# Issuing the raw expert weight loads of an attention and mixture-of-experts kernel on POOL's DMA queue

## The chip, the cores and the metric

The kernel runs on one core of one Trainium2 chip. The core has a TensorE for matrix products (PE in the rows), a VectorE (DVE), a ScalarE (ACT), a GpSimd (POOL) and a SyncE (SP), each with an instruction stream of its own that runs in program order, and 16 DMA engines that move data between HBM and the on-chip memory. SP and POOL can both issue DMAs; the rows call SP's sequencer SPq. The metric is the device time of one execution in microseconds (us), as the median over several executions.

## What is computed

Three stages follow one another: sparse attention (a local window and a few global keys) over 4 batches, 8 heads, 768 positions and a head size of 64; a dense layer pair 512 to 2048 to 512 with an ELU between; and a mixture of 8 experts, of which each token uses at most one. The last is what the change touches:

```python
def _moe2_ref(x, w_skip, w_gate, w1, w2):
    do_compute = x @ w_skip > 0
    out = x.copy()
    xc = x[do_compute]
    logits = xc @ w_gate
    e_idx = np.argmax(logits, axis=1)
    ...
    for e in range(E):                       # 8 experts
        mask = e_idx == e
        h = np.maximum(xc[mask] @ w1[e], 0.0)            # w1[e]: 512 x 1024
        y[mask] = gate_w[mask, None] * (h @ w2[e])       # w2[e]: 1024 x 512
    out[do_compute] = xc + y
    return out
```

All inputs are float32. The kernel makes each matrix product out of three float16 products (high part by high part, high by low, low by high).

## The kernel before

The 3072 tokens pass through attention and the dense pair in 8 groups `m` of 384 tokens; a group takes 16 steps `f` (128 of the 2048 hidden columns each). In a step `moe_h` makes `h` (L441), ACT and DVE make the ELU, ACT its high half `gs[:, 0]` (L451), POOL its low half (L452), and two steps later `moe_y` multiplies it by the second weight (L462). Each group is then routed (`route`): its rows are written to a table `xg` in HBM, 256 rows for each expert, by an indirect DMA that POOL issues (L586).

Experts come last. Their raw weights arrive in 64 loads of 512 KB (`ex_load`): for expert `e`, loads `k` = 0 to 3 are `w1`, 4 to 7 are `w2`. Two consecutive loads share a tile `er` of the pool `stage`, which has two buffers, so a pair of loads waits until the pair before the last has been worked up. `ex_prep` works a load up in two halves: ACT writes the scaled high part (L627), DVE the low part (L628) of `ew`. When `prep()` takes the first half of a load `k` it first calls `ex_load` for `k + 2`. The first 32 halves (experts 0 and 1) are worked up during group 7 of the dense pair, the rest in `ex_tail`.

In `ex_tail` steps run over `(e, f, tiles)`: first experts 0 to 3 with their first 128 tokens (32 steps), then experts 0 to 3 with their second 128 (32 steps), then experts 4 to 6 with 256 tokens at once, then expert 7 in two halves. A step is `ex_first` (L665, result `eh`), ACT and DVE make `ehs` (L667, L669), and two steps later `ex_second` (L681, result `eo`). A step goes with one half of `prep`, from expert 4 on with two; steps 32 to 41 have none. Tokens are fetched from `xg` by SP (`ex_gather`, L640, tile `yg`), split by DVE into `eyh` (L649, L650; one buffer) and turned by a transposing DMA that SP issues (`ex_tokens`, L651, tile `eyT`). After an expert's last step DVE makes the rows `eres` (L689) and their row numbers `ix` (L691), and POOL scatters them to the output (L692).

The framework's scheduler decides the order in which each engine's instructions stand, except for those pinned to program order (`self.pin`); waits are on semaphores, and an engine or a queue that waits holds back all that stands behind it.

Of the kernel before, what the change touches and what calls it, by code (L numbers as in the profile page):

```python
# [64 lines left out]
class Fast:  # L65
# [538 lines left out]
    def ex_load(self, e, k):  # L604
        nc = self.nc
        w1 = self.a["moe2_w1"][e].rearrange("(c p) f -> p c f", p=P)
        w2 = self.a["moe2_w2"][e].rearrange("(g c p) d -> p g c d", p=P, c=2)
        if k % 2 == 0:
            self.es = self.stage(f"er_{e}_{k}")
        r = self.es[:, k % 2]  # L610
        if k < 4:
            nc.sync.dma_start(r, w1[:, k])
        else:
            nc.sync.dma_start(r.rearrange("p (c d) -> p c d", c=2), w2[:, k - 4])
        self.er[(e, k)] = r

    def ex_prep(self, e, k, j):
# [581 lines left out]
```

## Time and profile before

| | |
|---|---|
| three runs | 863.15 us median (861.58 to 864.68) |
| the profiled execution | 864.38 us, of which the span of its instructions is 862.6 us |
| PE busy | 819.2 us, 95% of the span |
| DVE, ACT, POOL busy | 571.3, 532.1 and 173.5 us |
| mean granted TensorE clock | 0.981 of full speed |
| SP's DMA queue (hardware_dynamic) | 141.59 MB, 60.7% of 16 DMA engines' span |
| POOL's DMA queue (software_dynamic) | 5.99 MB, 1.9% |

Times in the rows count from the span's start. A row of the timeline gives the start, the length, the engine, the line, the operation and how often it is repeated; in brackets stands how long the engine was idle before, and who ended that. POOL's 64 weight loads do not exist yet: what POOL issues before are 24 scatters to `xg` and 16 to the output.

### The profile page before, as it was taken

To read this page: it belongs to the slowest core of one execution; us is meant where nothing else is said; L and a number is where in the kernel's file an instruction comes from. 1 tells how busy PE (TensorE), PEld (TensorE's weight loads), DVE (VectorE), ACT (ScalarE), POOL (GpSimd) and SP (SyncE) were. 2 spreads that over 40 slices of the span, in tenths; PEclk is the share of its full clock that TensorE was granted. 3 is DMA by queue.
4 is the path that set the end of the run, shared out by engine and by line. 5 is a ranking of instruction groups with operands and counts; after the bars stand their busy time and mean duration, and the time that the engine had idled before them with its cause. 6 is when DMAs were issued, how large, how long until landed. Compare 5 with 4: busy or idle time off the path is not lost.

```text
span 862.6 us, 17864 instructions
## 1 busy us (share of the span) xinstructions
PE 819.2 (95%) x6329; PEld 479.1 (56%) x6329; DVE 571.3 (66%) x1967; ACT 532.1 (62%) x1318; POOL 173.5 (20%) x201
## 2 busy tenths in 40 slices
PE   6998989999999999999999999999999889989995
PEld 5774444555555555555555555555555666756663
DVE  7997996575566576656656756542677865867832
ACT  4775766777766677776767776644766443545421
POOL 1002112123123211321321232232241111100010
PEclk9998998999999999999999999999999899999998
DMA  8998983544686486578547755420656796578810
GB/s 299 268 276 259 245 218 90 118 111 105 184 230 172 127 195 146 154 195 217 160 133 179 166 137 153 93 64 13 174 182 178 209 308 175 186 219 249 244 44 25
DMA packets 185395, 148.80 MB, mean 173 GB/s; under 512 B 152209, under 2 KB 154257, under 8 KB 181201
## 3 DMA queue, kind: packets, MB, share of 16 engines
q1 hardware_dynamic: 182096, 141.59, 60.7%
q0 software_dynamic: 3200, 5.99, 1.9%
q8 instruction: 51, 0.84, 0.4%
q14 instruction: 48, 0.39, 0.2%
HBM read 94.82 MB, written 21.08 MB: 134 GB/s over the span
## 4 chain that ended last, share of the span: by engine, by line
PE 72%; DVE 11%; DMA 9%; issue 3%; ACT 1%; POOL 1%; SPq 1%; DVEq 0%; POOLq 0%; ACTq 0%
PE h L441 25%; PE y L462 23%; PE eh L665 6%; PE eo L681 6%; PE s L241 5%; PE pv L326 5%; DMA eyT<-eyh 4%; DVE wt L410 1%; PE warm L356 1%; DVE w L418 1%; DMA er<-in_moe_w 1%; DVE ew L628 1%; DVE wt L411 1%; DMA pT<-ph 1%; DVE p L250 1%
## 5 line engine op out<-in xcount | busy, mean ns | idle before, releaser
L441 PE MATMUL h<-xT,w 128*128 128x384 f16 x1536 | 276.1, 330 | 3.9 <-DMA xT<-xs 3.0
L462 PE MATMUL y<-w,gs 128*128 128x512 f16 x1152 | 271.9, 380 | 1.1 <-POOL gs L452 1.0
L452 POOL TENSOR_TENSOR gs<-e,gs 128x384 f16<-128x384 f32 x128 | 123.3, 966 | 431.7 <-ACT gs L451 361.3
L441 PEld LDWEIGHTS <-w 128*128 128x128 f16 x1536 | 147.3, 99 | 107.0 <-issue 11.2
L462 PEld LDWEIGHTS <-gs 128*128 128x128 f16 x1152 | 109.8, 98 | 121.5 <-POOL gs L452 4.2
L448 DVE SCALAR_TENSOR_TENSOR e<-e,h 128x384 f32<-128x384 f32 x128 | 70.3, 550 | 108.4 <-ACT e L446 104.5
L451 ACT ACTIVATE gs<-e 128x384 f16<-128x384 f32 x128 | 66.7, 522 | 78.6 <-DVE e L448 77.4
L255 ACT ACTIVATE p<-p,st 128x232 f32<-128x232 f32 (+1 forms) x192 | 89.3, 466 | 40.2 <-DVE st L250 39.9
L665 PE MATMUL eh<-eyT,ew 128*128 128x128 f16 (+1 forms) x1248 | 104.7, 235 | 8.8 <-DMA eyT<-eyh 5.3
L665 PEld LDWEIGHTS <-ew 128*128 128x128 f16 x1248 | 90.0, 99 | 36.0 <-DMA eyT<-eyh 6.7
L628 DVE SCALAR_TENSOR_TENSOR ew<-er,ew 128x512 f16<-128x512 f32 x128 | 91.6, 729 | 26.6 <-ACT ew L627 26.2
L681 PE MATMUL eo<-ew,ehs 128*128 128x512 f16 x384 | 101.9, 383 | 3.2 <-ACT ehs L667 1.5
L445 ACT ACTIVATE e<-h 128x384 f32<-128x384 f32 x128 | 61.8, 483 | 65.5 <-PE h L441 52.5
L667 ACT ACTIVATE ehs<-eh 128x128 f16<-128x128 f32 (+1 forms) x104 | 31.3, 301 | 91.5 <-PE eh L665 91.5
L627 ACT ACTIVATE ew<-er 128x512 f16<-128x512 f32 x128 | 75.9, 620 | 11.3 <-DMA er<-in_moe_w 11.3
L250 DVE CUSTOM_DVE_ANT_0 p<-s,tab 128x232 f32<-128x232 f32 (+1 forms) x192 | 67.0, 376 | 20.4 <-PE s L241 18.6
L285 DVE TENSOR_TENSOR ph<-p,ph 128x464 f16<-128x464 f32 x68 | 42.8, 644 | 41.0 <-ACT ph L284 41.0
L446 ACT ACTIVATE e<-e 128x384 f32<-128x384 f32 x128 | 66.7, 521 | 2.6
L669 DVE SCALAR_TENSOR_TENSOR ehs<-eh,ehs 128x128 f16<-128x128 f32 (+1 forms) x104 | 33.0, 318 | 36.9 <-ACT ehs L667 35.2
L692 POOL DMA_INDIRECT out<-eres,ix x16 | 18.0, 1124 | 167.8 <-DVE ix L691 78.6
L681 PEld LDWEIGHTS <-ehs 128*128 128x128 f16 x384 | 34.6, 99 | 28.6 <-DVE ehs L669 3.0
L241 PE MATMUL s<-qh 64*128 64x232 f16 (+1 forms) x432 | 40.2, 256 | 4.0 <-DVE st L250 3.0
(171 smaller groups left out, 849.1 us busy)
## 6 DMA issues: line engine op xcount, KB each, us to landing
er<-in_moe_w SPq DMA_DIRECT2D x64, 512.0 KB
wr<-in_wf SPq DMA_DIRECT2D x16, 1024.0 KB
wc<-in_wf SPq DMA_DIRECT2D x16, 1024.0 KB
qk<-in_qk SPq DMA_DIRECT2D x20, 720.0 KB
out<-yt SPq DMA_DIRECT2D x24, 256.0 KB
rawv<-in_vp SPq DMA_DIRECT2D x21, 256.0 KB
xg<-zrow SPq DMA_DIRECT2D x16, 257.0 KB
yg<-xg SPq DMA_DIRECT2D x16, 257.0 KB
```

Of the source, the lines that this page charges most:

```text
L241: nc.tensor.matmul(sp[j], q[r, hp, KW:], k[r, hp, KW - w:KW], start=(x == 0), stop=(x == len(mm) - 1))
L250: nc.vector.tensor_tensor_reduce(pw[:, j, :], sp[j], self.tab[:, h, :] if i else self.tab0[:, h, :], -0.125, 3e38, ALU.add, ALU.min, st[:, ...
L255: nc.scalar.activation(pw[:, j, :], pw[:, j, :], AF.Exp, bias=st[:, 0, h:h + 1], scale=-1.0, accum_out=st[:, 1, h:h + 1])
L441: nc.tensor.matmul(hps, wi[:, s_, c, :], xT[:, x * ND + c, :], start=(n == 0), stop=(n == 3 * ND - 1))
L446: nc.scalar.activation(e, e, AF.Relu, scale=-1.0, bias=1.0)
L448: nc.vector.scalar_tensor_tensor(g, e, -HS, hps, ALU.mult, ALU.max, accum_out=self.gsum[:, m * NF + f:m * NF + f + 1])
L452: nc.gpsimd.tensor_tensor(gs[:, 1], g, gs[:, 0], ALU.subtract)
L462: nc.tensor.matmul(self.ys[m][t], gs[:, s_, t * P:(t + 1) * P], wo[:, x, :], start=(f == 0 and n == 0), stop=(f == NF - 1 and n == 2))
L627: self.pin(nc.scalar.activation(w[:, 0], r, AF.Copy, scale=sc))
L628: nc.vector.scalar_tensor_tensor(w[:, 1], r, sc, w[:, 0], ALU.mult, ALU.subtract, accum_out=self.esums[:, c:c + 1])
L665: nc.tensor.matmul(hps, l, r, start=(i == 0), stop=(i == len(mm) - 1))
L681: nc.tensor.matmul(self.eo[(e, t)], hs[:, s_, j * P:(j + 1) * P], self.ew[(e, 4 + f // 2, f % 2)][:, x, :], start=(f == 0 and n == 0), sto ...
```

## The change

Both DMA calls in `ex_load` are issued by POOL instead of SP. The 64 loads, their sizes, their buffers and everything else stay.

```diff
@@ def ex_load(self, e, k): @@
         r = self.es[:, k % 2]
         if k < 4:
-            nc.sync.dma_start(r, w1[:, k])
+            nc.gpsimd.dma_start(r, w1[:, k])
         else:
-            nc.sync.dma_start(r.rearrange("p (c d) -> p c d", c=2), w2[:, k - 4])
+            nc.gpsimd.dma_start(r.rearrange("p (c d) -> p c d", c=2), w2[:, k - 4])
         self.er[(e, k)] = r
```

The scheduler places the loads anew. The first place is POOL's stream in steps 9 to 12 of the dense pair's group 7, where the loads of expert 1 (`er_4`, `er_6`) now stand between the low halves `gs` of four steps:

```order
 L452 TENSOR_TENSOR gs_9_8180<-e_9_8176,gs_9_8180 128x384
+L614 DMA er_4_8228<-in_moe_w 128x2x512 x2
 L452 TENSOR_TENSOR gs_10_8225<-e_10_8221,gs_10_8225 128x384
 L452 TENSOR_TENSOR gs_11_8270<-e_11_8266,gs_11_8270 128x384
+L614 DMA er_6_8280<-in_moe_w 128x2x512 x2
 L452 TENSOR_TENSOR gs_12_8313<-e_12_8309,gs_12_8313 128x384
```

A pair of loads, with its wait for a free buffer, stands ahead of every other `gs`.

The second place is around steps 10 to 17 of `ex_tail`. On POOL, the last loads of expert 2 (`er_6_8748`) and the first of expert 3 (`er_0_8880`, `er_2_8971`) now stand among the scatters:

```order
+L614 DMA er_6_8748<-in_moe_w 128x2x512 x2
 L692 DMA out<-eres_0_8799,ix_0_8801 3072x512
 L586 DMA xg<-yt_8547,pos_8459 2048x514
 L586 DMA xg<-yt_8550,pos_8459 2048x514
 L586 DMA xg<-yt_8553,pos_8459 2048x514
+L612 DMA er_0_8880<-in_moe_w 128x1024 x2
+L612 DMA er_2_8971<-in_moe_w 128x1024 x2
 L692 DMA out<-eres_0_9003,ix_0_9005 3072x512
```

All four loads of `w1` of expert 3 come behind the group's three scatters to `xg`. On SP the same loads are gone from among the output writes (L593) and the first gather of the second tokens (`yg_1_9080`), which waits for those scatters:

```order
-L612 DMA er_0_8880<-in_moe_w 128x1024
 L593 DMA out<-yt_8547 128x512
 L593 DMA out<-yt_8550 128x512
 L593 DMA out<-yt_8553 128x512
-L612 DMA er_0_8880<-in_moe_w 128x1024
 L640 DMA yg_1_9080<-xg 128x514
-L612 DMA er_2_8971<-in_moe_w 128x1024 x2
 L640 DMA yg_1_9082<-xg 128x514
```

Before, the third and fourth load of expert 3 stood behind that gather's wait.

The third place is DVE's stream just before expert 4's first step, where its second 128 tokens are split (`eyh_1_10056`):

```order
 L669 SCALAR_TENSOR_TENSOR ehs_5_1_10073,esums<-eh_5_1_10060,ehs_5_1_10073 128x128
 L628 SCALAR_TENSOR_TENSOR ew_1_1_10076,esums<-er_0_9895,ew_1_1_10076 128x512
+L649 TENSOR_SCALAR eyh_1_10056<-yg_1_9903 128x512
 L669 SCALAR_TENSOR_TENSOR ehs_6_1_10095,esums<-eh_6_1_10082,ehs_6_1_10095 128x128
-L649 TENSOR_SCALAR eyh_1_10056<-yg_1_9903 128x512
+L650 SCALAR_TENSOR_TENSOR eyh_1_10056<-yg_1_9903,eyh_1_10056 128x512
 L628 SCALAR_TENSOR_TENSOR ew_2_0_10100,esums<-er_2_9995,ew_2_0_10100 128x512
-L650 SCALAR_TENSOR_TENSOR eyh_1_10056<-yg_1_9903,eyh_1_10056 128x512
 L669 SCALAR_TENSOR_TENSOR ehs_7_1_10119,esums<-eh_7_1_10106,ehs_7_1_10119 128x128
```

The split stands one `ehs` and one `ew` earlier; for experts 5 and 6 it moves ahead of one `ew` in the same way.

## Rows read from the trace of the kernel before

**Rows 1.** The page: busy us, share of the span and instructions of PE.
```profile
PE 819.2 (95%) x6329; PEld 479.1 (56%) x6329; DVE 571.3 (66%) x1967; ACT 532.1 (62%) x1318; POOL 173.5 (20%) x201
```

**Rows 2.** Windows: stretch, PE, PEld, DVE, ACT, POOL busy, granted clock, DMA share, GB/s.
```profile
664.00:690.00 26.00, 22.66 (x236) 15.28 (x233) 22.13 (x112) 14.28 (x40) 4.29 (x4) 0.87 0.72 193
690.00:720.00 30.00, 26.90 (x294) 18.56 (x293) 21.04 (x91) 14.31 (x38) 3.36 (x4) 1.00 0.86 281
758.00:780.00 22.00, 18.07 (x123) 12.05 (x121) 12.84 (x46) 9.44 (x21) 0.97 (x1) 0.92 0.75 198
```

**Rows 3.** Timeline of PE after its three longest idle stretches of the expert stage.
```profile
673.59 1.44 PE L665 MATMUL eh<-eyT,ew 128*128 128x128 f16 x12 [2.99 <-DVE ehs L669]
...
764.74 5.77 PE L665 MATMUL eh<-eyT,ew 128*128 128x256 f16 x36 [3.49 <-DMA eyT<-eyh]
...
807.75 1.49 PE L665 MATMUL eh<-eyT,ew 128*128 128x256 f16 x12 [1.86 <-DMA eyT<-eyh]
```

**Rows 4.** PE's waits from 690 to 720 us: total us, times, longest.
```profile
PE eo L681 <- ACT ehs L667: 1.5, 1, 1.5
PE eo L681 <- DVE ew L628: 1.0, 2, 0.6
```

**Rows 5.** The chain that ended last, its transfers: start, us, what.
```profile
653.24 2.56 DMA eyT<-eyh
...
657.76 4.20 DMA eyT<-eyh
...
760.62 4.07 DMA eyT<-eyh
...
791.98 4.59 DMA yg<-xg
...
802.31 5.40 DMA eyT<-eyh
```

**Rows 6.** Timeline of SP's queue: issues of the weight loads (a row's length includes waits).
```profile
657.15 0.35 SPq L612 DMA_DIRECT2D er<-in_moe_w  x1
...
687.75 0.34 SPq L612 DMA_DIRECT2D er<-in_moe_w  x1
...
697.34 0.84 SPq L612 DMA_DIRECT2D er<-in_moe_w  x2
...
736.57 6.63 SPq L614 DMA_DIRECT2D er<-in_moe_w  x4
...
757.65 0.89 SPq L614 DMA_DIRECT2D er<-in_moe_w  x2
...
784.16 6.57 SPq L614 DMA_DIRECT2D er<-in_moe_w  x4
```

**Rows 7.** Line 692, POOL's scatters to the output: ns min/median/max, and landing.
```profile
L692 POOL DMA_INDIRECT out<-eres,ix x16: 971/976/1469, 686.0 to 853.8; - x16
...
DMA to landing us min/median/max: 2.2/3.6/6.0
```

**Rows 8.** The tile er, its issues by SP: ns min/median/max, first and last start.
```profile
L612 SPq DMA_DIRECT2D er<-in_moe_w x32: 327/395/972, 512.9 to 803.6; - x32
```

**Rows 9.** Timeline of ACT: first halves of two loads worked up.
```profile
692.57 0.62 ACT L627 ACTIVATE ew<-er 128x512 f16<-128x512 f32 x1
...
741.78 0.62 ACT L627 ACTIVATE ew<-er 128x512 f16<-128x512 f32 x1
```

**Rows 10.** ACT's waits from 690 to 720 us: total us, times, longest.
```profile
ACT ew L627 <- DMA er<-in_moe_w: 6.4, 3, 3.1
```

**Rows 11.** Timeline of POOL: a low half of the dense pair, the last scatter.
```profile
642.17 0.92 POOL L452 TENSOR_TENSOR gs<-e,gs 128x384 f16<-128x384 f32 x1 [2.29 <-ACT gs L451]
...
690.34 0.97 POOL L586 DMA_INDIRECT xg<-yt,pos  x1 [0.30 <-ACT ehs L667]
```

**Rows 12.** Timeline of PE: the first product that uses that low half.
```profile
650.72 2.11 PE L462 MATMUL y<-w,gs 128*128 128x512 f16 x9
```

## The prediction

> **What bounds the kernel now.** I read the page first: PE is busy for 95% of the span [rows 1], so a transfer matters only where PE stands still for it. The windows then show where that is. Until 664 us the loads come into being beside a PE that works through; behind it, PE is busy for 22.66 of 26 us in 664 to 690, 26.90 of 30 in 690 to 720, 18.07 of 22 in 758 to 780 [rows 2]. Third, the timeline of PE names the idle stretches: 2.99 us before 673.59, ended by DVE; 3.49 us before 764.74 and 1.86 us before 807.75, both ended by a turned token tile `eyT` [rows 3]. Between 690 and 720 it loses 1.5 us to ACT and 1.0 us to DVE [rows 4], and behind both stands ACT, which waits 6.4 us for the raw weights themselves [rows 10]. Two of the stretches also cost clock: the granted clock is 0.87 and 0.92 of full speed in their windows [rows 2], which is a part of each at 1.2 instead of 2.4 GHz. After 1.86 us idle there is none of that: 12 products of 256 columns take 1.49 us, after 3.49 us 36 of them take 5.77, or 1.3 us more than 3 x 1.49 [rows 3].
>
> So all that can be won is some 2.99 + 2.5 + 3.49 + 1.86 = 10.8 us of standstill, and a few us of clock behind it.
>
> **What the transfers wait for.** The chain of waits shows four transposes and a gather. The transpose at 653.24 lands in 2.56 us; nothing else had been issued for some time. At 657.76 one takes 4.20, at 760.62 one takes 4.07, at 802.31 one takes 5.40, and the gather at 791.98 takes 4.59 [rows 5]. Ahead of each, SP had issued weight loads of 512 KB to the same queue: at 657.15, two from 757.65, four from 784.16 on [rows 6]. I read the excess over 2.56 us as time behind those loads.
>
> **The change, term by term.**
>
> *Removed from SP:* 64 issues of about 0.4 us [rows 8], with their waits. SP is not waited for by itself, so this is worth nothing directly; what counts is what then goes ahead sooner.
>
> *The stretch before 673.59.* It ends on DVE, which first had to split four token tiles through one buffer, each after the landing of the one before. The second transpose can lose at most 4.20 - 2.56 = 1.64 us [rows 5]. Much of the rest of that wait is DVE's work on the last group's rows, which stays. Bounds 0 and 1.6; I take 0.5, because DVE has other work to fill the wait with. The clock stays lost.
>
> *Expert 3, 690 to 720.* Here a gain and a loss meet. The gain: the third and fourth load, at 697.34 on SP [rows 6] behind a gather that waited for the scatters, no longer stand behind it. The loss: the first load, at 687.75 on SP, stands behind three scatters on POOL, the last at 690.34 for 0.97 us [rows 11], so at 691.3. Its landing I estimate from the scatter to the output: 3.6 us median for 256 KB [rows 7], and 0.9 us more for another 256 KB at the window's 281 GB/s [rows 2], together 4.5 us; so 695.8, where ACT wants it at 692.57 [rows 9]. ACT then stands for 3.2 us, as it did before at its longest (3.1 [rows 10]), which cost PE 1.5 [rows 4]. One such wait in place of two stalls that cost 2.5: a gain of 1.0. Bounds: all 2.5 gained, or 2 us lost if the queue is held up as in the longest landing, 6.0 us instead of 3.6 [rows 7].
>
> *Expert 4, the stretch before 764.74.* The transpose at 760.62 can lose 4.07 - 2.56 = 1.5 us [rows 5], and DVE makes its input one `ew` sooner. I take 1.5; bounds 0 (loads and transposes still share the DMA engines) and 3.5. If the idle time falls under 2 us the 1.3 us of clock [rows 3] come back too; I leave that out, since 2.0 lies between 1.86 that kept the clock and 2.99 that did not.
>
> *Expert 6, the stretch before 807.75.* Gather and transpose exceed 2.56 by 2.0 and 2.8 us [rows 5]; 1.86 are wanted. I take all 1.86; bounds 0 and 1.86.
>
> *Added to POOL:* 64 issues at 0.976 us, at worst 1.469, by the nearest row, a scatter of 128 rows [rows 7]; a direct load may cost less, down to SP's 0.4 [rows 8]. In the dense pair's group 7 a pair stands ahead of every other `gs`: 2 x 0.976 = 2.0 us in front of a POOL instruction of 0.92 us. The low half at 642.17 is first used at 650.72 [rows 11, 12], so it can be 7.6 us late. Cost 0. Were that cover gone, each of the 8 pairs would cost PE up to 2 us. In the expert stage POOL has nothing but scatters, which hold nobody until their rows or buffers are used again.
>
> *Cadence.* A pair of loads may start when its buffer comes free, and has to be there four halves later; with a step of 1.3 us that is 5.2 us, as from SP's issue at 736.57 to ACT at 741.78 [rows 6, 9]. By my estimate of 4.5 us POOL's loads fit, with 0.7 us to spare. I charge 0.5 us in all for ACT waits that PE feels.
>
> The sum: 0.5 + 1.0 + 1.5 + 1.9 - 0.5 = 4.4 us. The profiled execution took 864.38 us, so 860.0 for it; it lies 1.2 us above the median of 863.15, so **858.8 us** for the median.
>
> **Rivals.**
>
> *The loads are still in the way.* A transpose that no longer stands behind a load in its queue meets the same 512 KB on the same DMA engines, busy for 72 to 86% of these windows [rows 2]; if they take turns, it lands no earlier. For this: the bytes do not change. Against it: the third and fourth load of expert 3 stood still for a reason that has nothing to do with bytes. Then 1.0 - 0.5 remain: 862.6 us. The Trainium skill speaks for this rival: by "DMA: Bandwidth & Descriptors", section "Issuing engines are not separate DMA queues", DMAs of all issuing engines run on the same 16 engines and interleave, and spreading them saves only issue time; by that the change would be worth nothing. No row of before shows a load and a transpose in two queues.
>
> *POOL's loads come late (slower).* If a load needs more than the 5.2 us of the cadence, ACT falls behind by the excess with each pair, while steps last 1.3 us. There are 10 such pairs (two of expert 2, four of 3, two of 4, two of 5). The point of decision is a landing of 5.2 us. The longest scatter took 6.0 [rows 7], with the larger load 6.9: 1.7 us too much. If that holds for half of the pairs, 5 x 1.7 = 8.5 us are lost, and with 4.4 - 0.5 still won at the other places the time is 863.15 - 3.9 + 8.5 = 867.8. If it holds for all 10, 876. For it: scatters took from 2.2 to 6.0 us to land, and generating one took up to 1.469 us instead of 0.971 [rows 7]. Against it: the queue that they competed with carried these very loads, and would now be emptier. The Trainium skill has a rule on this side: "SBUF — State Buffer", the box on the "DVE blocks DMA" trap, says that GpSimd cannot write the descriptors of its DMAs while DVE runs an operation in a two-port mode, and gives 620 ns that become about 3100. By that factor of five a load would be some 2.5 us late, an estimate of 25 us over ten pairs. The rows agree that generation stretches, by 0.5 us at most [rows 7].
>
> *POOL waits in front of PE.* A `gs` late by more than its 7.6 us is only possible if a pair of loads waits for its buffer that long; the buffer comes free in the step before, so I give this no chance of its own.
>
> **How the numbers follow.** The forecast gets 0.50, the loads still in the way 0.27, late loads 0.23. A measurement of this kernel can tell about 0.3% (2.6 us) from no change, so faster means below 860.6 and slower above 865.7: 0.50, 0.27 and 0.23. Low end: the upper bounds at experts 3 and 4 with the clock (1.5 + 2.0 + 1.3 more) and another 2 us of the first stretch's clock, 858.8 - 6.8 = 852. High end: late loads at half of the pairs, 868. The likeliest case by itself lies between 855 and 861.
>
> **What would show it.** Right: the transposes of `eyT` land in 2.6 to 3 us; the idle stretch before 807.75 is gone and that before 764.74 is near 2 us; `gs` never ends a wait of PE for more than 0.3 us; POOL's issues take about 1 us. Wrong: `eyT` still takes 4 us and more (the first rival), or the waits of ACT for `er`, 6.4 us in 690 to 720 before, grow past 15 us over the expert stage and PE's waits for ACT and DVE with them (the second). The place to look at first is expert 3, where the new order puts four loads behind three scatters.

## The result and the profile after

The change makes the kernel slower: 871.7 us median (867.94 to 879.2, 13 runs) against 863.15 us (857.82 to 867.34, 13 runs), a ratio of 1.0112 with a 95% interval of 1.0081 to 1.0142. The forecast was 858.8 us. A cost in us below is the difference of two medians, here 8.6 us; the ratio is made from all runs and can say about 1 us otherwise.

The profiled execution took 871.25 us, with a span of 869.5 us, 6.9 us more than before. The page of it, with the busy time of each engine and the DMA queues (packets, MB, share of 16 engines):

```profile
PE 822.5 (95%) x6329; PEld 481.0 (55%) x6329; DVE 571.8 (66%) x1967; ACT 532.5 (61%) x1318; POOL 215.7 (25%) x265
...
q1 hardware_dynamic: 168784, 108.04, 48.3%
q0 software_dynamic: 12416, 39.55, 13.3%
```

The bytes have gone over: POOL's queue moves 39.55 MB where it moved 5.99. Of the 6.9 us PE is busy for 3.3, with the same products [rows 1], and stands still for 3.6. The windows of the expert stage tell where (columns as in [rows 2]):

```profile
664.00:690.00 26.00, 19.24 (x207) 12.97 (x205) 21.91 (x109) 13.31 (x36) 6.27 (x8) 0.93 0.61 172
690.00:720.00 30.00, 26.15 (x276) 18.65 (x275) 20.47 (x88) 14.51 (x37) 12.14 (x16) 0.94 0.80 268
720.00:758.00 38.00, 35.84 (x389) 25.69 (x387) 23.00 (x101) 15.16 (x42) 8.59 (x11) 0.96 0.51 157
758.00:780.00 22.00, 17.48 (x149) 11.72 (x148) 13.14 (x51) 8.66 (x21) 5.50 (x8) 0.84 0.65 184
```

PE is busy for 19.24 us where it was for 22.66, 26.15 for 26.90 and 17.48 for 18.07 [rows 2]. In 720 to 758 it had worked through at full clock, by the row of before,

```profile
720.00:758.00 38.00, 38.00 (x435) 27.74 (x433) 26.92 (x116) 18.73 (x50) 5.11 (x4) 1.00 0.60 188
```

and now loses 2.16 us; the granted clock falls in three of the four windows and rises in the first. In these four windows PE stands 6.9 us longer than before; outside them it stands 3.3 us less, which leaves the 3.6 of the whole span.

What DVE waits for, in 590 to 870 us (total, times, longest), shows the engine on which it starts:

```profile
DVE eyh L649 <- DMA eyT<-eyh: 12.8, 6, 4.1
...
DVE eyh L649 <- issue: 7.0, 2, 4.2
```

DVE stands 12.8 us before it may write the next token tile, because the transpose of the one before has not landed. In the trace of before it was 5.5 us,

```profile
DVE eyh L649 <- DMA eyT<-eyh: 5.5, 6, 1.6
```

and no wait of `eyh` was put down to issue (a wait for which the profile shows no releaser). The timeline, engine by engine, shows one such stretch whole, the second transpose:

```profile
656.38 1.11 POOL L612 DMA_DIRECT2D er<-in_moe_w  x2 [2.06 <-DVE ew L628]
656.71 1.23 SPq L651 DMA_TRANSPOSE eyT<-eyh  x1
664.02 0.43 DVE L649 TENSOR_SCALAR eyh<-yg 128x512 f16<-128x512 f32 x1 [4.14 <-DMA eyT<-eyh]
666.55 0.60 PE L462 MATMUL y<-w,gs 128*128 128x512 f16 x2 [1.91 <-ACT gs L451]
675.59 1.44 PE L665 MATMUL eh<-eyT,ew 128*128 128x128 f16 x12 [3.00 <-DVE ehs L669]
```

POOL issues two loads at 656.38 and SP the transpose at 656.71. It holds its buffer until 664.02, or 7.3 us, where it took 4.20 [rows 5]. Behind DVE's wait stand the rows of the dense pair's last group, so ACT has `gs` late and PE stands 1.91 us at 666.55. The product that began at 673.59 [rows 3] begins at 675.59. Around 720 the same thing happens to the sixth transpose:

```profile
716.84 1.15 POOL L612 DMA_DIRECT2D er<-in_moe_w  x2 [0.22 <-issue]
718.70 1.23 SPq L651 DMA_TRANSPOSE eyT<-eyh  x1
723.71 0.43 DVE L649 TENSOR_SCALAR eyh<-yg 128x512 f16<-128x512 f32 x1 [2.77 <-issue]
725.61 0.59 PE L681 MATMUL eo<-ew,ehs 128*128 128x512 f16 x2 [2.15 <-DVE ew L628]
```

Before, it was issued at 714.43 and DVE wrote the next tile at 717.32:

```profile
717.32 0.43 DVE L649 TENSOR_SCALAR eyh<-yg 128x512 f16<-128x512 f32 x1 [0.67 <-DMA eyT<-eyh]
```

From issue to the next write of the buffer it is 5.0 us now and was 2.9, and the converted weights that stand behind it in DVE's stream come 2.15 us late for PE. The third place is expert 3's first load:

```profile
693.96 1.15 POOL L612 DMA_DIRECT2D er<-in_moe_w  x2
700.78 0.63 ACT L627 ACTIVATE ew<-er 128x512 f16<-128x512 f32 x1 [5.63 <-DMA er<-in_moe_w]
701.63 0.61 PE L681 MATMUL eo<-ew,ehs 128*128 128x512 f16 x2 [2.85 <-ACT ehs L667]
```

It leaves POOL behind the third scatter (issued at 693.00), and ACT stands 5.63 us for it.

Not every transpose is late. The loads leave POOL in pairs, and a transpose between two pairs meets none of them. Counted in the traces from issue to the last data packet, six of the 16 transposes end 1.2 to 2.9 us later than before (the second, fourth, sixth, ninth, eleventh and thirteenth) and six end 0.3 to 2.5 us sooner (the third, seventh, eighth, tenth, twelfth and fourteenth). Two of the sooner ones stand in the chain of waits:

```profile
771.12 2.73 DMA eyT<-eyh
...
813.90 2.73 DMA eyT<-eyh
```

They are the tenth and the fourteenth, which had taken 4.07 and 5.40 us [rows 5], and PE's own waits for a turned tile fall from 5.3 to 2.1 us (590 to 870 us). What grows is the time for which their predecessors hold the token buffer: 6.7 us for the ninth, where it was 3.9, and 4.6 for the thirteenth, where it was 2.8.

### The profile page after: what moved, and what is told of

Read it like the earlier page. It is cut to its first block, busy times and chain, and to the rows that moved or that the text cites. A ratio compares the mean times of both kernels' runs of the same rounds, so it can differ in the third digit from the quotient of the medians.

```text
span 869.5 us, 17882 instructions
## 1 busy us (share of the span) xinstructions
PE 822.5 (95%) x6329; PEld 481.0 (55%) x6329; DVE 571.8 (66%) x1967; ACT 532.5 (61%) x1318; POOL 215.7 (25%) x265
## 3 DMA queue, kind: packets, MB, share of 16 engines
q0 software_dynamic: 12416, 39.55, 13.3%
## 5 line engine op out<-in xcount | busy, mean ns | idle before, releaser
L627 ACT ACTIVATE ew<-er 128x512 f16<-128x512 f32 x128 | 75.8, 620 | 19.8 <-DMA er<-in_moe_w 19.7
L250 DVE CUSTOM_DVE_ANT_0 p<-s,tab 128x232 f32<-128x232 f32 (+1 forms) x192 | 67.0, 377 | 21.5 <-PE s L241 19.7
L326 PE MATMUL pv<-vv,pT 128*128 128x64 f16 x888 | 41.4, 195 | 0.6 <-DVE sq L340 0.4
```

What stands on the lines that cost most here:

```text
L250: nc.vector.tensor_tensor_reduce(pw[:, j, :], sp[j], self.tab[:, h, :] if i else self.tab0[:, h, :], -0.125, 3e38, ALU.add, ALU.min, st[:, ...
L627: self.pin(nc.scalar.activation(w[:, 0], r, AF.Copy, scale=sc))
```

## The experiments

Five theories were on trial. **Theory 1**: in SP's one queue a load and a token transpose followed each other; in two queues the loads leave in pairs next to a transpose and the transposes land late. **Theory 2**: expert 3's first loads are late because they stand behind three scatters on POOL. **Theory 3**: each load costs the same through POOL, whatever stands beside it, 8.55/64 us each. **Theory 4**: DVE's rows, which the scheduler put in a slightly other order, cost the time. **Theory 5**: a load of another queue holds a transpose up for longer than the same load in SP's own queue.

### Which expert's loads cost the time

Each kernel sends part of the loads through POOL and leaves the rest with SP. The edit is always this one, with another condition (here the loads of experts 0 and 1, 16 of the 64):

```diff
-        r = self.es[:, k % 2]
+        r, q = self.es[:, k % 2], (nc.gpsimd if e < 2 else nc.sync)
         if k < 4:
-            nc.sync.dma_start(r, w1[:, k])
+            q.dma_start(r, w1[:, k])
...
```

> Only the 16 loads of experts 0 and 1 go through POOL's queue. Theory 1 (a transpose in SP's queue and a load in POOL's queue take turns on the DMA engines, so the transposes that split tokens wait for land late and hold DVE) and theory 2 (the first loads of expert 3 stand behind three scatters on POOL) both expect no change: these loads are issued before 650 us, ahead of the first token transposes and scatters of the tail; 0 +- 1 us. Theory 3 (each load through POOL costs the same, 8.55 us over 64 loads) expects 16/64 of the loss, +2.1 us.

Measured: 860.33 us against 860.85, ratio 0.999 (0.997 to 1.0011). No change, so theory 3 falls: sixteen loads through POOL cost nothing where no token transpose is near.

```diff
+        r, q = self.es[:, k % 2], (nc.gpsimd if e == 2 else nc.sync)
```

> Only the 8 loads of expert 2 go through POOL. Theory 1: they meet the first four token transposes and the three of the last group, so the second token transpose lands 3 us later than before, the last low half of group 7 and the last group's logits come late: +2 to +4 us. Theory 2: 0. Theory 3: +1.1 us.

Measured: 868.11 us, 1.009 (1.0062 to 1.0118), 7.3 us more, for eight loads. It is more than theory 1 had said.

```diff
+        r, q = self.es[:, k % 2], (nc.gpsimd if e == 3 else nc.sync)
```

> Only the 8 loads of expert 3 go through POOL. Theory 2: the first load lands at about 700 us instead of before 693, ACT stands more than 5 us for it, PE about 3 us plus 2 us at the low clock, against 2.5 us of standstill that go: +2 to +4 us. Theory 1 alone: the transposes from 709 on meet four loads, up to +2 us. Theory 3: +1.1 us.

Measured: 861.77 us, 1.0006 (0.9986 to 1.0026). No change (the interval leaves room for up to 2.2 us), so theory 2 falls as the main cause, though its wait is there: ACT's longest wait for `er` is 4.8 us in this run and PE stands 2.5 us once. That wait stands largely in place of others: PE's waits from 690 to 720 us add up to 3.6 us, against 3.1 before.

```diff
+        r, q = self.es[:, k % 2], (nc.gpsimd if e >= 4 else nc.sync)
```

> Only the 32 loads of experts 4 to 7 go through POOL. Theories 1 and 2: the changed kernel lost 1 us net behind 735 us, so 0 to +2 us. Theory 3: half of the loss, +4.3 us.

Measured: 869.93 us, 1.0098 (1.0067 to 1.013), 9.1 us more. A miss for every theory as it stood: I had put the price of the transposes at expert 2 alone. Experts 2 and 4 to 7 are the ones with token transposes among their loads in SP's order; experts 0, 1 and 3 have none among theirs. The parts (7.3 and 9.1) add up to more than the whole (8.6), so they cover each other in part.

### Sixteen loads against the other forty-eight

In the order of SP's stream of the kernel before, the loads that stand between two transposes are nearly all among the first four of experts 2, 4, 6 and 7. One kernel sends just these 16 through POOL, the other just the other 48:

```diff
+        r, q = self.es[:, k % 2], (nc.gpsimd if e in (2, 4, 6, 7) and k < 4 else nc.sync)
```

> Only 16 of the 64 loads go through POOL: the first four of experts 2, 4, 6 and 7, which in the kernel before stand between token transposes in SP's queue. Theory 1 (the transposes lose the order that SP's queue gave them: the loads now leave in pairs next to a transpose): the whole loss or nearly, +6 to +10 us. Theory 3 (each load through POOL costs the same): a quarter, +2.1 us. Theory 4 (the scheduler's other order of DVE's rows costs it) has the same change of DVE's order as the full change and says +8.

Measured: 868.64 us against 860.34, 1.0102 (1.0082 to 1.0122). In the trace DVE's rows have moved in three of the five places in which the full change moves them, so this run does not separate theory 4 from theory 1.

```diff
+        r, q = self.es[:, k % 2], (nc.gpsimd if not (e in (2, 4, 6, 7) and k < 4) else nc.sync)
```

> The other 48 loads go through POOL, and the 16 that stand between token transposes stay with SP. Theory 1: no loss, -3 to +2 us. Theory 3: three quarters, +6.4 us.

Measured: 862.9 us, 1.0028 (1.001 to 1.0046); 2.6 us more, a little over what was expected. So a quarter of the loads carries nearly the whole loss (8.3 us) and three quarters carry 2.6. The timeline of the kernel with the 16 shows the second transpose again:

```profile
657.86 1.15 POOL L612 DMA_DIRECT2D er<-in_moe_w  x2 [2.21 <-DVE ew L628]
658.19 1.23 SPq L651 DMA_TRANSPOSE eyT<-eyh  x1
667.05 0.43 DVE L649 TENSOR_SCALAR eyh<-yg 128x512 f16<-128x512 f32 x1 [5.70 <-issue]
669.58 2.93 PE L462 MATMUL y<-w,gs 128*128 128x512 f16 x6 [5.41 <-ACT gs L451]
```

And the kernel with the 48, where SP again issues one load, the transpose, the other load:

```profile
657.06 0.34 SPq L612 DMA_DIRECT2D er<-in_moe_w  x1
657.66 1.23 SPq L651 DMA_TRANSPOSE eyT<-eyh  x1
658.94 0.58 SPq L612 DMA_DIRECT2D er<-in_moe_w  x1
661.93 0.43 DVE L649 TENSOR_SCALAR eyh<-yg 128x512 f16<-128x512 f32 x1 [0.80 <-DMA eyT<-eyh]
```

From issue to the next write of the buffer it is 8.9 us with the 16, and 4.3 us with the 48. The 48 still send some pairs beside a transpose, which may be where their 2.6 us come from: the fifth, ninth and eleventh hold the buffer for 4.8, 5.4 and 5.7 us, where it was 3.7, 3.9 and 4.9. ACT's waits for the loads don't follow the number of loads in POOL's queue: 18.0 us in total with 16 loads through POOL, 9.6 us with 48, against 11.3 us with none.

### One load, a pair, four loads

```diff
+        r, q = self.es[:, k % 2], (nc.gpsimd if (e, k) == (2, 1) else nc.sync)
```

> One load of the 64 goes through POOL: the second of expert 2, which stood right behind the second token transpose in SP's queue and now may leave before it. DVE's order of rows is that of the kernel before. Theory 1: this transpose lands at 6 to 7 us after its issue where it took 4.2, and the time grows by +3 to +7 us. Theory 3: +0.13 us, no change. Theory 4 (DVE's order): no change.

Measured: 863.65 us against 860.34, 1.0028 (1.0008 to 1.0048). One load of 64 costs 3.3 us (2.4 by the ratio), and in the traces the rows of DVE, ACT and PE stand in the same order as before: theory 4 isn't needed here, and theory 3 is out once more. The transpose holds its buffer from 659.29 to 665.15, 5.9 us, a little under what was expected.

```diff
+        r, q = self.es[:, k % 2], (nc.gpsimd if e == 2 and k < 2 else nc.sync)
```

> The pair of loads that opens expert 2 goes through POOL, where the earlier run moved its second load alone. Theory 1: with two loads issued next to it the second token transpose takes 7 to 9 us to the next write of its buffer (one load: 5.85, none moved: 4.2), and the time grows by +5 to +8 us, nearly the whole of what expert 2's eight loads cost (+7.3). If the load that passes the transpose is all that counts: the +2.4 to +3.3 us of the one load again.

Measured: 863.62 us against 860.44, 1.0038 (1.0011 to 1.0065). The transpose is as late as expected, 8.2 us:

```profile
656.52 1.15 POOL L612 DMA_DIRECT2D er<-in_moe_w  x2 [2.20 <-DVE ew L628]
656.85 1.23 SPq L651 DMA_TRANSPOSE eyT<-eyh  x1
...
665.01 0.43 DVE L649 TENSOR_SCALAR eyh<-yg 128x512 f16<-128x512 f32 x1 [5.00 <-issue]
```

but the time grows by 3.2 us only, as with the one load. PE's waits in 640 to 760 of this run say why (total, times, longest):

```profile
PE y L462 <- ACT gs L451: 4.7, 1, 4.7
...
PE eh L665 <- DVE ehs L669: 0.8, 1, 0.8
```

PE stands 4.7 us earlier, at the dense pair's last rows, and then hardly at the place where it had stood 2.99 us [rows 3]: a late transpose here is partly paid by a wait that was there anyhow. The other six loads of expert 2 make up the way from 3.2 to 7.3 us; that part wasn't taken apart further.

```diff
+        r, q = self.es[:, k % 2], (nc.gpsimd if e == 4 and k < 4 else nc.sync)
```

> Four loads go through POOL: the first four of expert 4, which in SP's queue stand behind the fifth, the sixth and the seventh token transpose. DVE's rows stand in the order of the kernel before. Theory 1: the sixth transpose takes 5 to 5.3 us to the next write of its buffer instead of 2.9, PE stands some 2 us more near 720, and with the clock the time grows by +2 to +5 us. Theory 4 (DVE's order): no change. Theory 3: +0.5 us.

Measured: 864.14 us against 860.44, 1.0051 (1.0027 to 1.0075), again with the rows of DVE, ACT and PE in the order of before. So five loads in two places cost 3.3 and 3.7 us without any help from theory 4; as a part of the rest it isn't excluded. The timeline has the whole chain:

```profile
708.92 1.13 POOL L612 DMA_DIRECT2D er<-in_moe_w  x2 [0.28 <-DVE ew L628]
...
710.09 1.23 SPq L651 DMA_TRANSPOSE eyT<-eyh  x1
715.67 0.43 DVE L649 TENSOR_SCALAR eyh<-yg 128x512 f16<-128x512 f32 x1 [3.35 <-issue]
717.57 0.93 PE L681 MATMUL eo<-ew,ehs 128*128 128x512 f16 x2 [2.73 <-DVE ew L628]
```

A pair of loads, a transpose that takes 5.6 us instead of 2.9, DVE held for 3.35 us, PE for 2.73.

### The two transfers by themselves

This kernel leaves the whole computation out and writes zeros. Six times over it turns a tile of 128 x 1024 float16, as the kernel does, from SP, alone or with one or two loads of 512 KB beside it (`v` names the variant, `q` the queue of its `n` loads):

```python
        for v, q, n, turn, row in VARIANTS:
            ...
            for y in range(n):
                e = getattr(nc, q)
                if row == 4:
                    d = e.dma_start(r[y], w1[:, i % 4])
                ...
                pin(d)
            if turn:
                t = sb.tile([P, 8, P], F16, tag="t", name=f"t{v}_{i}")
                pin(nc.sync.dma_start_transpose(t, h))
```

> A measurement by itself that leaves the whole computation out (the output is zeros): a token-sized transpose from SP, alone and behind or beside one or two loads of 512 KB that are issued just ahead of it by SP, by POOL or by ACT. A load has 128 packets of 4096 bytes at 159 ns, 1.27 us on 16 DMA engines. Theory 1, in which it's the bytes ahead of the transpose that cost and not the queue: alone 2.3 to 2.6 us, one load +1.0 to +1.5, two loads +2.2 to +2.8, and within 0.5 us the same from SP, POOL and ACT. Theory 5 (a load of POOL's queue, or of any queue beside SP's, holds up a transpose for longer than the same load in SP's own queue): beside POOL's loads the transpose ends over 1 us later than behind SP's.

The DMA issues of it, each with the median us from issue to landing (`none` alone, `sp`, `pool` and `act` behind or beside one load in that engine's queue, a name said twice for two loads):

```profile
tnone<-hnone SPq DMA_TRANSPOSE x6, 3.1
tsp<-hsp SPq DMA_TRANSPOSE x6, 4.2
tpool<-hpool SPq DMA_TRANSPOSE x6, 4.9
tspsp<-hspsp SPq DMA_TRANSPOSE x6, 5.3
tpoolpool<-hpoolpool SPq DMA_TRANSPOSE x6, 6.1
tpoolhalf<-hpoolhalf SPq DMA_TRANSPOSE x6, 6.4
tact<-hact SPq DMA_TRANSPOSE x6, 4.2
tactact<-hactact SPq DMA_TRANSPOSE x6, 5.8
```

A load ahead in SP's queue costs a transpose 1.1 us, two cost 2.2, counted from the transpose's own issue. Beside POOL's queue it is 1.8 and 3.0, beside ACT's 1.1 and 2.7. Alone it takes 3.1 us, more than the 2.3 to 2.6 expected. But the transposes do not start at the same point. In SP's queue one is issued behind all its loads; beside POOL's it is issued almost together with the first of them:

```profile
40.44 0.81 SPq L1160 DMA_DIRECT2D rspsp<-in_moe_w  x2
41.35 1.23 SPq L1168 DMA_TRANSPOSE tspsp<-hspsp  x1
...
47.66 1.05 POOL L1160 DMA_DIRECT2D rpoolpool<-in_moe_w  x2 [12.19 <-DVE rpoolpool L1154]
47.83 1.23 SPq L1168 DMA_TRANSPOSE tpoolpool<-hpoolpool  x1
```

The median distance is 0.92 us behind SP's two loads, 0.17 beside POOL's and 0.43 beside ACT's. Counted from the first load's issue to the landing of the transpose, the medians are 4.6, 5.0 and 4.7 us with one load of SP, POOL and ACT, and 6.2, 6.3 and 6.2 with two. So theory 1 holds: it is the bytes that cost, whichever queue they are in. Of the 0.7 to 0.8 us that POOL's queue seems to add, 0.27 and 0.75 are the transpose's earlier start; 0.4 and 0.1 are left, and theory 5 is not borne out. Loads in rows of 2 KB (`poolhalf`) help nothing. Above all, a transpose that leaves the loads' queue does not land sooner: it starts sooner and waits longer.

### Three attempts to take the cost away

Twelve of the 16 loads wait, by a copy of one column on POOL, for the transpose that stood ahead of them in SP's queue:

```diff
+        r, q = self.es[:, k % 2], (nc.gpsimd if e in (2, 4, 6, 7) and k < 4 else nc.sync); (e, k) in BEHIND and nc.gpsimd.tensor_copy(r[:, 0:1], ...)
...
+BEHIND = {(2, 1): (1, 0), (2, 2): (2, 0), (2, 3): (3, 0), (4, 1): (1, 1), (4, 2): (2, 1), (4, 3): (2, 1),
+          (6, 1): (5, 0), (6, 2): (5, 0), (6, 3): (5, 1), (7, 1): (6, 0), (7, 2): (6, 0), (7, 3): (6, 1)}
```

> The same 16 loads through POOL as in the run that moved only these, but 12 of them wait, through a copy of one column on POOL ahead of each, for the token transpose that stood in front of them in SP's queue. Theory 1 (the lost order costs): most of the +8.6 us comes back, +0 to +4 us against the kernel before, and the second transpose lands at 4 to 5 us again. Theory 5 alone (a load in POOL's queue holds a transpose up for longer, whatever the order): +6 to +9 us stay.

Measured: 876.14 us against 861.26, 1.0169 (1.0137 to 1.0202). A miss. The second and the sixth transpose are back at 5.0 and 3.7 us, as theory 1 has it, but the copies hold the loads longer than SP's queue did. There the load behind the second transpose left 1.28 us after the transpose's issue (659.04 after 657.76); here it waits until the transpose has landed and leaves 5.4 us after its issue (663.58 after 658.14). ACT's waits for the loads grow to 28.6 us, from 18.0 with the 16 loads alone, and PE's for `eyT` to 9.7, from 3.4. By line and tile, the rows of PE, ACT, DVE and SP stand in the order of the kernel with the 16 loads, and only POOL's differ. The order of before was not restored but overdone, so the run decides nothing on the total.

Two buffers for the token rows, so that DVE need not wait for a transpose before it writes the next tile; first with all loads on SP, then with all on POOL:

```diff
-            w = self.xp.tile([P, 2, DM], F16, tag="xw", name=f"ew_{e}_{k}_{j}", bufs=32)
+            w = self.xp.tile([P, 2, DM], F16, tag="xw", name=f"ew_{e}_{k}_{j}", bufs=30)
...
-        yh = self.mp.tile([P, 2, DM], F16, tag="yh", name=f"eyh_{e}_{t}", bufs=1)
+        yh = self.xp.tile([P, 2, DM], F16, tag="eyh", name=f"eyh_{e}_{t}", bufs=2)
```

> The kernel before with two buffers for the token rows that a transpose reads (two of the 32 buffers of converted weights are given up for it), so that DVE need not wait for one transpose before it writes the next token tile. If DVE's wait for the transpose (5.5 us in the trace of before) is a cost of the kernel before as well: -1 to -5 us. If the waits are hidden, or 30 buffers of weights are too few: 0 to +3 us.

Measured: 875.62 us against 861.26, 1.0162 (1.0128 to 1.0197). A miss: the two buffers, with the 30 that are left and the scheduler's new order, cost more than DVE's wait; which of these costs it isn't shown.

> The same two buffers in the changed kernel (all loads through POOL). If the late transposes reach PE through DVE's wait for the one buffer, the loss against the two-buffer kernel with loads on SP is 0 to +4 us instead of +8.6. If PE waits for the transposes themselves, +6 to +9 us stay.

Measured: 878.9 us, 1.0202 (1.0169 to 1.0234) against the kernel before, and 3.3 us over the two-buffer kernel with loads on SP. Here the same move of all 64 loads costs 3.3 us where it costs 8.6 with one buffer. That speaks for the one buffer as the way to PE, but the two kernels differ from the original in DVE's order too, so it supports and doesn't prove. No run beat the kernel before.

## Why the prediction was wrong

**The step that failed** is the reading of the transfers: "I read the excess over 2.56 us as time behind those loads", and from it, under what is removed from SP, that "what counts is what then goes ahead sooner". The excess is time behind the loads' bytes, not behind their place in the queue, so it goes wherever the loads go. Two of the named transposes did land sooner, at 2.73 us for 4.07 and 5.40, for no load leaves just ahead of them any more. But pairs now leave beside others: the second, of which a gain was expected, holds the buffer for 7.3 us instead of 4.2, and the sixth and the ninth, for which the sum has nothing, hold it for 5.0 instead of 2.9 and 6.7 instead of 3.9. The chain of waits of before has nine transposes, not four; the other five had taken 2.80 to 4.76 us, and the sixth (2.80) and the ninth (2.95) were among them.

The measurement by itself has like figures: 3.1 us alone and 4.2 with one load ahead in SP's queue, an excess of 1.1 us where [rows 5] has 1.64; moved to POOL's queue the same load makes it 4.9. The Trainium skill, "DMA: Bandwidth & Descriptors", section "Issuing engines are not separate DMA queues", says that DMAs of all engines run on the same 16 engines and interleave, and that only issue time is saved. The runs agree with the first half. They go past the second: here spreading cost 8.6 us, for SP's queue had also kept the next load behind the transpose.

**Sign and rivals.** The first rival had the cause, that loads and transposes still meet on the same DMA engines, and a wrong price: it said that a transpose "lands no earlier", worth 862.6 us. Those that meet a pair land later. The order of [rows 6], one load, transpose, next load, let a transpose meet one load; POOL, which doesn't wait for DVE's token tiles, sends two. The slower rival was nearest in time (867.8) with another mechanism. Its sign is in the trace (ACT's waits for `er` are 19.7 us over the expert stage, past the 15 named, and were 11.3 before), but the kernel with 48 loads through POOL has 9.6 us of such waits and costs 2.6, the one with 16 has 18.0 and costs 8.3, and the one with the eight loads of expert 2 has 9.4 and costs 7.3: ACT's waits follow neither the number of loads in POOL's queue nor the loss. That this rival came near the measured time was luck.

**Term by term.**

- *The stretch before 673.59*, -0.5 us: it came out +2.00, by the product that now begins at 675.59. The second transpose did not lose its 1.64 us; it took 3.1 more.
- *Expert 3*, -1.0: the first load left POOL at 693.96 instead of the estimated 691.3, since the last scatter came at 693.00, and ACT had it 6.8 us later instead of the estimated 4.5, so that ACT stood 5.63 us instead of 3.2. By itself this place costs nothing in the end (1.0006 with only expert 3 moved), so the term was mis-sized by about 1 us and is not where the loss is.
- *Expert 4, before 764.74*, -1.5: the 3.49 us are now three stretches of 2.72, 0.48 and 1.32 us, 4.5 in all, with the clock at 0.84 in the window for 0.92 [rows 2, 3]. Only the last of them ends on `eyT`, as the 3.49 did; the other two end on DVE, behind the ninth transpose.
- *Expert 6, before 807.75*, -1.86: two stretches of 0.53 and 0.75 us remain, so 0.6 were won. The transpose that the term named lands in 2.73 us; the one before it, at 807.59, takes 4.52 us by the chain of waits. The gather's 4.59 us had been set against the 2.56 of a transpose, which no row supports. The second stretch in the timeline:

```profile
816.68 0.49 PE L665 MATMUL eh<-eyT,ew 128*128 128x256 f16 x3 [0.75 <-DMA eyT<-eyh]
```

- *POOL's issues*, 0: right. An issue takes 0.55 or 0.72 us, under the 0.976 assumed, and `gs` ended one wait of PE, of 0.44 us, a little past the 0.3 that the prediction allowed; before, it ended one of 0.3. The rows of the loads' tile, with min, median and max of an issue in ns and of the landing:

```profile
L612 POOL DMA_DIRECT2D er<-in_moe_w x32: 528/550/599, 513.6 to 815.3; - x32
L614 POOL DMA_DIRECT2D er<-in_moe_w x32: 704/723/798, 608.3 to 823.4; - x32
...
DMA to landing us min/median/max: 3.6/4.7/8.0
```

- *Cadence*, +0.5: the estimated landing of 4.5 us was good as a median (4.7), the longest is 8.0. The Trainium skill's box on the "DVE blocks DMA" trap ("SBUF — State Buffer"), drawn on for this rival, has DMAs issued by GpSimd wait for their descriptors behind DVE; the 620 and 3100 ns stand in the section behind the box, "A bandwidth-pool intuition that's wrong (but worth ruling out)". The longest issue here is 1.1 times the median and the longest landing 1.7 times, so no row of this case shows a factor of five, and [rows 7] do not say that DVE stretched the one scatter of 1.469 us.
- *Not in the sum at all*: the window from 720 to 758, in which nothing was to be won, and nothing was looked for to be lost. It went from 38.00 us busy to 35.84, through the sixth transpose, which had taken 2.9 us and so was not on the list.

**What stays open.** The price of a late transpose depends on what wait of PE lies there already, so parts and whole don't add up; the six later loads of expert 2 weren't taken apart; and the lost order was shown by which loads carry the loss, not by putting it back. No run has SP itself send a pair ahead of a transpose, which would show the order without POOL's queue inside the kernel.

## What to carry to other kernels

A queue that holds one transfer behind another also keeps a third one back: before loads are moved to an empty queue, look in the issuing order for the small transfers that something waits for, also for those that are quick today, and ask which loads will now leave beside them. To spread issues over queues saves what the issuing engine loses, and nothing of what the bytes cost. A transfer that holds the only buffer of an in-order engine is the one to shield: all that stands behind it in that engine's stream inherits its delay.

## What the runs showed of the hardware

A transpose that starts sooner, in a queue of its own, does not land sooner: with two loads of 512 KB it lands 6.2 us after the first load's issue behind them in SP's queue, 6.3 beside POOL's and 6.2 beside ACT's, though it is issued 0.92, 0.17 and 0.43 us after that load. And where the profile puts DVE's wait for the token buffer down to issue, DVE can start well behind the transpose's data: in the kernel with 16 loads the trace's last data packet of that transpose ends 6.8 us after its issue, the last 4-byte packet of SP's queue 7.7, and DVE goes on at 8.9. From 7.7 to 8.8 the trace has a 16-KB packet of a queue that the page calls instruction (q8); the kernels with the pair and with the eight loads of expert 2 show the same, but in the changed kernel DVE goes on 0.2 us before such a packet ends, and the measurement by itself, in which TensorE has no work, has no packet of q8. Whether DVE waited for it wasn't tried.
